# Decoding fp64 weights on chip: a Prelu that carries the sign in bit 28, and a join of one shift

## Chip, cores and metric

The kernel runs on one core of one Trainium2 chip. The metric is the device time of one launch in microseconds (us). Beside it stands one execution recorded by the hardware profiler, with its own time.

## What is computed

An RWKV-6 attention block (4 batches, 8 heads, 768 tokens, head width 48), and on its output a two-layer block with the gate h·erf(softplus(h)):

```python
for t in range(S):
    kt, vt, rt, wt = (k[:, :, t], v[:, :, t], r[:, :, t], w[:, :, t])
    cur = np.einsum('bhd,bhe->bhde', u[None] * kt, vt)
    y[:, :, t] = np.einsum('bhd,bhde->bhe', rt, state + cur)
    state = wt[:, :, :, None] * state + np.einsum('bhd,bhe->bhde', kt, vt)
...
h = x @ w_in                      # 3072 tokens, 384 -> 2048
sp = np.maximum(h, 0.0) + np.log1p(np.exp(-np.abs(h)))
g = h * erf(sp)
return (g @ w_out).astype(np.float32)
```

The two weight matrices arrive as fp64, as the inputs hold them (`w_in` and `w_out` are random numbers divided by a float64 square root), so the kernel turns them into fp32 on the chip.

## The kernel before

**Steps.** The outer loop runs over `n_steps` = 12 steps `s`; each takes 128 tokens of two batches. Step `s` does its attention, and between the pieces of that the two-layer block of earlier steps is put: the first layer of step s-1 (`hidden`, matmuls of L777, whose PSUM tile "m" ScalarE copies out at L786), softplus and erf of it (L759 and L762 for the first steps, L733 and L737 later), and the second layer of step s-3 (`project`, L809, later `project_fast`, L885). The "m" tiles are two, taken in turn: a piece of L777 can start only when the copy L786 of the piece two before it is done.

**Attention of the first steps.** For s < 5 the products inside a block of 64 tokens are built in six levels, `level` 1 to 6. At each level TensorE forms products (L452) into a PSUM tile "pp", VectorE scales the operands for the next level (`scale` at L263), and takes the products into `own` (L668 at level 1, a predicated copy L464 at levels 2 to 5, two ScalarE copies L471 at level 6). Then come a transpose of K (L680), its copy by ScalarE (`kT`, L684), the state's products (L538), additions on VectorE and GpSimd (L710 to L715), and `through_state` (L512 on TensorE, L519 to L522 on ScalarE), whose result `xT` is completed by six small DMAs (L526, three issued by SP, three by ScalarE). The first layer of that step can start when those have landed.

**Order.** The order on each engine is the order in which the program issues (`manual_schedule`). After each level `place(n)` is called, and it puts there what the tables say: pieces of the two-layer block, stages of softplus, erf and their product (`advance`, `STAGES`), and stages of the conversion.

**The conversion.** `convert` is a generator that takes letters. There are 16 pieces of weights, each 128 partitions x 2 x 384: pieces 0 to 7 are `w_in`, 8 to 15 are `w_out`. For one piece i:

- "l", `load(i)`: a 768 KB DMA on SP's queue into a `words` buffer of 32-bit words (3 buffers), the low and the high word of each fp64 next to each other.
- "s", `scale(i)`: ScalarE reads the high words as fp32, multiplies by 2^-112 and writes `base` into the PSUM tile "pp1" (L212); this lowers the exponent field. Then it reads the low words as unsigned integers, multiplies by 2^-29 and writes `rest` (L214, 2 buffers).
- "j", which is `shift` ("h") and then `join` ("o"): VectorE shifts `base` left by 3 bits in place (L220). The sign falls out at the top, so a second VectorE instruction (L228) takes the sign bit from `words`, ors it with the shifted bits and writes the weights. Then GpSimd adds `rest` to them (L232).

`CONVERT` says at which place of which of the steps 0 to 3 which letters run. In step 1 the `h` of piece 2 stands at place 0 ("hl"), and its `o` is issued at level 2 between VectorE's scaling L263 and its taking L464 (`behind(None)`, `BEHIND_SCALING = "os"`). The PSUM tile "pp1" is one: `scale(i+1)` can write it only after VectorE has read piece i out of it. While the conversion runs, all other users of "pp" take "pp0".

Of the kernel before, what the change touches and what calls it, by code (L numbers as in the profile page):

```python
# [11 lines left out]
FP32 = mybir.dt.float32  # L12
I32 = mybir.dt.int32
U32 = mybir.dt.uint32
AF = mybir.ActivationFunctionType
ALU = mybir.AluOpType
# [45 lines left out]
def kernel(  # L62
# [14 lines left out]
    nc = tc.nc  # L77
    PSUM = bass.MemoryType.PSUM

    n_steps, _, _, JP, C = rkw.shape  # L80
# [4 lines left out]
    _, NT, DM = w_out.shape  # L85
# [43 lines left out]
    turns = {"next": 0, "converting": False}  # L129
# [55 lines left out]
    def convert(weights):  # L185

        held = {}

        def load(i):
            if i >= len(weights):
                return
            dst, src = weights[i]
            if src.dtype == FP32:
                nc.sync.dma_start(out=dst, in_=src)
                return
            words = wide.tile([P, 2, DM, 2], I32, name="words", bufs=3)
            nc.sync.dma_start(
                out=words[:].rearrange("p i n two -> p i (n two)"), in_=src.bitcast(I32)  # L200
            )
            held[i] = [words]

        def scale(i):
            if i in held:
                words = held[i][0]
                low, high = words[:, :, :, 0], words[:, :, :, 1]
                base = ps_p.tile([P, 2, NP * C], FP32, name="pp1")[:, :, :DM]
                rest = wide.tile([P, 2, DM], I32, name="rest", bufs=2)


                nc.scalar.mul(out=base, in_=high.bitcast(FP32), mul=2.0**-112)  # L212

                nc.scalar.mul(out=rest[:], in_=low.bitcast(U32), mul=2.0**-29)  # L214
                held[i] += [base.bitcast(I32), rest]

        def shift(i):
            if i in held:
                bits = held[i][1]
                nc.vector.tensor_scalar(  # L220
                    out=bits, in0=bits, scalar1=3, scalar2=None, op0=ALU.logical_shift_left
                )

        def join(i):
            if i in held:
                words, bits, rest = held.pop(i)
                into = weights[i][0].bitcast(I32)
                nc.vector.scalar_tensor_tensor(  # L228
                    out=into, in0=words[:, :, :, 1], scalar=-(1 << 31), in1=bits,
                    op0=ALU.bitwise_and, op1=ALU.bitwise_or,  # L230
                )
                nc.gpsimd.tensor_tensor(out=into, in0=into, in1=rest[:], op=ALU.add)  # L232

        stages = {"l": load, "s": scale, "h": shift, "o": join}
        done = dict.fromkeys(stages, 0)
        for _ in range(3):
            load(done["l"])
            done["l"] += 1
        while True:
            what = yield  # L240
            for stage in {"j": "ho"}.get(what, what):
                stages[stage](done[stage])
                done[stage] += 1
            if weights[0][1].dtype != FP32:
                turns["converting"] = 0 < done["s"] and done["o"] < len(weights)
                turns["next"] = 0

    def rows(e, n=D):
# [723 lines left out]
    def run_late(s, tokens, following=None):  # L972
# [26 lines left out]

    CONVERT = (  # L1000
        ("", "", "", "", "", "s", "jls", "j", "sl"),
        ("hl", "jsl", "jsl", "jsl", "jl", "sj", "", "", "sl"),
        ("jsl", "jsl", "jsl", "jsl", "jl", "sj", "s"),
        ("js", "j"),
    )

    BEHIND_SCALING = "os"

    STAGES = {
        1: (0, 0, 0, 0, 0, 0, 1, 0), 2: (1, 0, 0, 0, 0, 0, 1, 1), 3: (1, 2, 1, 0, 0, 2, 1, 1)  # L1010
# [10 lines left out]
    with tc.manual_schedule(  # L1021
# [9 lines left out]
        for _ in prepare(0):  # L1031
            pass
        conversion = convert(
            [
                (into[:, f : f + 2, :], given[:, f : f + 2, :])
# [6 lines left out]
        for s in range(n_steps):  # L1042
# [39 lines left out]
            def behind(n=0):  # L1082
                if n is not None:
                    convert_at(LOG + 2)
                    return
                for what in BEHIND_SCALING:
                    conversion.send(what)
# [6 lines left out]
        s = n_steps  # L1094
# [104 lines left out]
```

## Time and profile before

| | |
|---|---|
| median of 3 runs | 599.53 us (597.93 to 599.68) |
| the profiled execution, own time | 598.5 us |
| its span | 596.3 us, with 2.2 us around it |
| TensorE (PE) matmuls busy | 584.7 us, 98% |
| VectorE (DVE) busy | 440.1 us, 74% |
| ScalarE (ACT) busy | 361.8 us, 61% |
| GpSimd (POOL) busy | 274.5 us, 46% |
| L212, high words scaled | 16 x 888 ns (median), from 25.4 to 108 us |
| L214, low words scaled | 16 x 915 ns |
| L220, shift | 16 x 966 ns |
| L228, sign and or | 16 x 954 ns |
| L232, GpSimd's addition | 16 x 2.1 to 2.3 us |

A timeline line gives the start, the length, the engine, the source line, the operation, out<-in with the shape, and how many instructions are merged in it; in brackets stands how long the engine was idle before it, and what the profile takes for the releaser. "PEld" is TensorE's loading of weights, "SPq" and "ACTq" are the queues of SP and ScalarE (issues of DMAs). Where several things released a wait, the line names the one that came last before the start, which need not be the true one.

### The profile page before, as it was taken

The page shows a single profiled execution, that of the slowest core. Times are in us where ns is not written, and L with a number is a line of the kernel's source. Part 1 is how long each engine was busy: PE and PEld are TensorE (multiplying, and loading weights), DVE is VectorE, ACT ScalarE, POOL GpSimd, SP SyncE. Part 2 cuts the span into 40 slices and gives each one's busy share as a digit, 9 for nine tenths or more (in the row PEclk, how much of TensorE's full clock was granted, in tenths as well). Part 3 has the DMA queues.
Part 4 walks back from the last instruction along what each step waited for, and adds up shares of the span by engine and source line. Part 5 has one row for each costly group of instructions (what it writes and reads, how often), then busy time and mean ns, then how long its engine had stood idle before and what let it go on. Part 6 is the DMA issues. An engine that isn't in the chain of part 4 may idle for free.

```text
span 596.3 us, 16645 instructions
## 1 busy us (share of the span) xinstructions
PE 584.7 (98%) x7290; PEld 501.7 (84%) x7290; DVE 440.1 (74%) x516; ACT 361.8 (61%) x473; POOL 274.5 (46%) x296
## 2 busy tenths in 40 slices
PE   8889999999999999999999999999999999999997
PEld 7667788678758758898898898898898898898997
DVE  5688598799996799799799799799799525023140
ACT  2547788717534398765765666666666664746710
POOL 4348365610588549749449449449459000000000
PEclk9999999999999999999999999999999999999999
DMA  8377381541315324334334335334331300000000
GB/s 320 124 278 234 118 290 58 217 141 20 134 38 159 66 95 168 71 108 169 72 107 168 73 106 169 73 107 134 71 107 54 71 9 26 2 21 13 2 27 26
DMA packets 51376, 63.33 MB, mean 106 GB/s; under 512 B 34920, under 2 KB 40296, under 8 KB 49896
## 3 DMA queue, kind: packets, MB, share of 16 engines
q1 hardware_dynamic: 50824, 62.03, 32.3%
q8 instruction: 57, 0.93, 0.6%
q10 hardware_dynamic: 480, 0.25, 0.2%
q14 instruction: 15, 0.12, 0.1%
HBM read 52.39 MB, written 8.69 MB: 102 GB/s over the span
## 4 chain that ended last, share of the span: by engine, by line
PE 88%; DVE 6%; issue 2%; ACT 2%; DMA 1%; POOL 1%; SPq 0%; DVEq 0%; ACTq 0%; POOLq 0%
PE m L777 40%; PE m L885 28%; PE m L809 8%; PE pp L452 6%; PE y L486 2%; DVE in L263 2%; PE pp L538 1%; PE y L512 1%; DMA in<-in_rkw 1%; PE pp L680 1%; DVE sums L367 1%; DVE words L381 1%; DVE own L464 1%; ACT rk L292 1%; DVE w_in_sb L228 0%
## 5 line engine op out<-in xcount | busy, mean ns | idle before, releaser
L777 PE MATMUL m<-xT,w_in_sb 128*128 128x256 f32 x1152 | 257.3, 382 | 2.3 <-DVE w_in_sb L228 1.3
L777 PEld LDWEIGHTS m<-xT,w_in_sb 128*128 128x128 f32 x1152 | 216.0, 190 | 34.5 <-issue 3.7
L786 ACT COPY h<-m 128x512 f32<-128x512 f32 x96 | 55.6, 580 | 84.2 <-PE m L777 84.1
L263 DVE TENSOR_TENSOR in<-in,tot_sb 128x1024 f32<-128x1024 f32 (+1 forms) x60 | 78.3, 1305 | 24.9 <-PE pp L452 23.8
L377 POOL TENSOR_TENSOR rk<-words 128x528 f32<-128x528 f32 (+3 forms) x28 | 41.6, 1485 | 91.4 <-DVE sums L367 81.0
L381 POOL TENSOR_TENSOR words<-words,rest 128x528 f32<-128x528 f32 (+10 forms) x77 | 79.1, 1027 | 6.0
L809 PE MATMUL m<-w_out_sb,h 128*128 128x384 f32 x192 | 64.3, 491 | 0.0
L809 PEld LDWEIGHTS m<-w_out_sb,h 128*128 128x128 f32 x192 | 35.7, 190 | 23.6
L885 PE MATMUL m<-mixed,h 128*128 128x192 f32 x288 | 51.1, 331 | 0.0
L885 PE MATMUL m<-w_out_sb,h 128*128 128x192 f32 x288 | 50.3, 329 | 0.0
L733 ACT ACT_TABLE_LOAD x36 | 46.2, 1283 | 2.4 <-issue 1.7
L885 PEld LDWEIGHTS m<-w_out_sb,h 128*128 128x128 f32 x288 | 46.9, 190 | 0.5
L885 PEld LDWEIGHTS m<-mixed,h 128*128 128x128 f32 x288 | 46.6, 190 | 0.9
L737 ACT ACT_TABLE_LOAD x36 | 46.2, 1283 | 1.7 <-DVE room L868 1.1
L452 PEld LDWEIGHTS pp<-in 48*64 48x64 f32 (+1 forms) x2368 | 34.0, 125 | 14.8 <-issue 8.1
L885 PE MATMUL m<-w_out_sb,room 128*128 128x192 f32 x256 | 44.2, 326 | 0.0
L452 PE MATMUL pp<-in 48*64 48x64 f32 (+1 forms) x2368 | 38.7, 212 | 4.0 <-issue 1.8
L315 POOL TENSOR_TENSOR tot_sb<-tot_sb 128x256 f32<-128x256 f32 (+4 forms) x60 | 40.4, 674 | 4.5
L885 PEld LDWEIGHTS m<-w_out_sb,room 128*128 128x128 f32 x256 | 42.0, 190 | 0.0
L742 DVE TENSOR_TENSOR h<-h,y 128x1024 f32<-128x1024 f32 x17 | 20.7, 1215 | 28.3 <-ACT y L737 28.2
L733 ACT ACTIVATE room<-h 128x1024 f32<-128x1024 f32 x36 | 38.1, 1057 | 0.4
L742 DVE TENSOR_TENSOR h<-h,pp 128x1024 f32<-128x1024 f32 x19 | 23.1, 1213 | 19.3 <-ACT pp L737 19.2
(123 smaller groups left out, 826.3 us busy)
## 6 DMA issues: line engine op xcount, KB each, us to landing
in<-in_rkw SPq DMA_DIRECT2D x11, 1024.0 KB, 5.1
words<-in_moe_w_in SPq DMA_DIRECT2D x8, 768.0 KB, 5.5
words<-in_moe_w_out SPq DMA_DIRECT2D x8, 768.0 KB, 4.6
words<-in_rk_rows SPq DMA_DIRECT2D x8, 768.0 KB, 6.2
w<-in_rkw SPq DMA_DIRECT2D x11, 512.0 KB, 7.0
v<-in_v SPq DMA_DIRECT2D x12, 384.0 KB, 6.0
out<-o SPq DMA_DIRECT2D x24, 192.0 KB, 2.4
rest<-in_w_rows SPq DMA_DIRECT2D x8, 384.0 KB, 5.0
```

The costliest lines, as they stand in the source:

```text
L263: nc.vector.tensor_mul(halves, halves, view(tots[level - 1], 0, [[1, n], [2, nb], [0, half]]))
L315: nc.gpsimd.tensor_mul(new, pair[:, :, 0], pair[:, :, 1])
L377: engine.tensor_mul(terms[n], r[:, :, n:], k[:, :, : near - n])
L381: engine.tensor_mul(k[:, :, :m], k[:, :, :m], w[:, :, n : n + m])
L452: nc.tensor.matmul(pp[s0 : s0 + m, e, n, :m], lhsT=rk[rows(e), 1, n, s0 : s0 + m], rhs=rk[rows(e), 0, n, t0 : t0 + m], start=True, stop=True,)
L733: nc.scalar.activation(sp_room, chunks[0], AF.Softplus)
L737: nc.scalar.activation(at, sp_room, AF.Erf)
L742: nc.vector.tensor_mul(h, h, at)
L777: nc.tensor.matmul(ps[:, ff, :], lhsT=w_in_sb[:, g * FG + f + ff, kk * P : (kk + 1) * P], rhs=xT[:, kk, :], start=kk == 0, stop=kk == KT - 1,)
L786: nc.scalar.copy(h[:, f : f + FT, :], ps[:])
L809: nc.tensor.matmul(ps[j][:], lhsT=gs[g][:, f, j * C : (j + 1) * C], rhs=w_out_sb[:, g * FG + f, :], start=g + f == 0, stop=g == NG - 1 and ...
L885: nc.tensor.matmul(to, lhsT=a[:, f], rhs=b[:, f], start=start and f == 0, stop=f == FG - 1, skip_group_check=True,)
```

## The change

Per piece, `scale` writes the high words with the activation function Prelu instead of a plain multiplication: the input is multiplied by 2^-112, positive values pass as they are, negative ones are multiplied by alpha = -2^32. A negative word so becomes a positive number whose exponent field is 32 higher, which sets bit 28. A shift left by 3 then moves bit 28 into the place of the sign. `shift` and the sign-taking instruction go; `join` is one shift that reads "pp1" and writes the weights; `words` is no longer read by VectorE. The letters h and o go, "hl" becomes "l", and "os" becomes "js".

```diff
-                nc.scalar.mul(out=base, in_=high.bitcast(FP32), mul=2.0**-112)
+                nc.scalar.activation(
+                    base, high.bitcast(FP32), AF.Prelu, scale=2.0**-112, alpha=-(2.0**32)
+                )
                 nc.scalar.mul(out=rest[:], in_=low.bitcast(U32), mul=2.0**-29)
                 held[i] += [base.bitcast(I32), rest]
-        def shift(i):
-            if i in held:
-                bits = held[i][1]
-                nc.vector.tensor_scalar(
-                    out=bits, in0=bits, scalar1=3, scalar2=None, op0=ALU.logical_shift_left
-                )
         def join(i):
             if i in held:
-                words, bits, rest = held.pop(i)
+                _, bits, rest = held.pop(i)
                 into = weights[i][0].bitcast(I32)
-                nc.vector.scalar_tensor_tensor(
-                    out=into, in0=words[:, :, :, 1], scalar=-(1 << 31), in1=bits,
-                    op0=ALU.bitwise_and, op1=ALU.bitwise_or,
-                )
+                nc.vector.tensor_scalar(
+                    out=into, in0=bits, scalar1=3, scalar2=None, op0=ALU.logical_shift_left
+                )
                 nc.gpsimd.tensor_tensor(out=into, in0=into, in1=rest[:], op=ALU.add)
-        stages = {"l": load, "s": scale, "h": shift, "o": join}
+        stages = {"l": load, "s": scale, "j": join}
...
-            for stage in {"j": "ho"}.get(what, what):
+            for stage in what:
...
-                turns["converting"] = 0 < done["s"] and done["o"] < len(weights)
+                turns["converting"] = 0 < done["s"] and done["j"] < len(weights)
...
-        ("hl", "jsl", "jsl", "jsl", "jl", "sj", "", "", "sl"),
+        ("l", "jsl", "jsl", "jsl", "jl", "sj", "", "", "sl"),
...
-    BEHIND_SCALING = "os"
+    BEHIND_SCALING = "js"
```

## The prediction, made before the changed kernel was run

> **What bounds the kernel now.** I read first the busy shares and the chain that ended last, on the profile's page:
>
> ```profile
> PE 584.7 (98%) x7290; PEld 501.7 (84%) x7290; DVE 440.1 (74%) x516; ACT 361.8 (61%) x473; POOL 274.5 (46%) x296
> PE 88%; DVE 6%; issue 2%; ACT 2%; DMA 1%; POOL 1%; SPq 0%; DVEq 0%; ACTq 0%; POOLq 0%
> ```
>
> TensorE works 584.7 of 596.3 us and carries 88% of the chain; 11.6 us of the span are left in which it idles. A change on VectorE can pay only there. The conversion lies at 25 to 118 us, so the next view is TensorE's timeline from 30 us on: which gaps it has and what ended them. There are four that matter:
>
> ```profile
> 34.40 3.27 PE L777 MATMUL m<-xT,w_in_sb 128*128 128x256 f32 x12 [1.26 <-DVE w_in_sb L228]
> ...
> 42.33 1.16 PE L452 MATMUL pp<-in 48*64 48x64 f32 x64 [0.77 <-DVE own L464]
> ...
> 69.32 3.14 PE L777 MATMUL m<-xT,w_in_sb 128*128 128x256 f32 x12 [0.98 <-DMA xT<-y]
> ...
> 76.53 1.16 PE L452 MATMUL pp<-in 48*64 48x64 f32 x64 [0.19 <-DVE own L464]
> 77.62 2.86 PE L777 MATMUL m<-xT,w_in_sb 128*128 128x256 f32 x12
> ```
>
> Together 3.2 us (one more, 0.48 us at 51.70, is put down to issue alone). From 77.6 us to the end of TensorE's work there is one more, 0.33 us at 172 us, behind a VectorE chain that itself starts at TensorE's L538 at 146 us: if TensorE comes later, so does that chain. So a delay of TensorE before 77 us reaches the end whole, and so does a gain.
>
> The first gap is put down to the join L228, which ended at 34.28. I don't believe that: this L777 reads piece 0 of the weights, which GpSimd finished at 30.26, and `xT`, whose DMAs were issued at 32.17 and took 1.7 to 2.1 us to land, so about 34.2. The third gap has the same form (issue 67.05, matmul 69.32, 2.27 us; here 2.23 us) and names the DMA.
>
> The last view is ScalarE's timeline about the last gap:
>
> ```profile
> 67.06 2.06 ACTq L526 DMA_DIRECT2D xT<-y  x3
> 69.22 0.86 ACT L212 ACTIVATE pp<-words 128x768 f32<-128x768 f32 x1 [1.92 <-DVE own L668]
> 70.01 0.88 ACT L214 ACTIVATE rest<-words 128x768 int32<-128x768 uint32 x1
> 70.80 0.57 ACT L786 COPY h<-m 128x512 f32<-128x512 f32 x1
> 72.10 0.89 ACT L212 ACTIVATE pp<-words 128x768 f32<-128x768 f32 x1 [0.73 <-DVE w_out_sb L228]
> 72.91 0.92 ACT L214 ACTIVATE rest<-words 128x768 int32<-128x768 uint32 x1
> 73.85 1.28 ACT L762 ACT_TABLE_LOAD   x1
> 75.14 1.91 ACT L762 ACTIVATE room<-room 128x2048 f32<-128x2048 f32 x1
> 76.96 0.57 ACT L786 COPY h<-m 128x512 f32<-128x512 f32 x1
> ```
>
> The copy L786 that ends at 77.53 frees the "m" tile that TensorE's L777 takes at 77.62. There is no slack in that pair: whatever makes this copy late stops TensorE.
>
> **What the Trainium skill says.** "ScalarE: Activation LUTs", section "Table sets: the hidden batching unit": functions are loaded in sets, and the cheap ones found in every set as filler are relu, copy, identity and abs; Prelu is not in that list. Its section "What ACT_TABLE_LOAD costs" gives 1283 ns a load, which is what the 85 loads here show (mean 1283), and 186 + 0.833·N ns for an ACTIVATE with immediate operands plus 93 ns for each per-partition operand: 826 ns for N = 768, against 888 measured for L212. "ScalarE activation tables: per-element evaluation and per-set limits", section "What a function is on this engine": with the same operands an ACTIVATE costs the same whichever table it reads. No run here shows a Prelu. "VectorE: DVE Perf Modes", section "Why PSUM operands drop a tier": an fp32 operation with a PSUM operand runs at one element a cycle. The trace agrees: the shift L220 takes 966 ns for 768 elements.
>
> **Part 1, one VectorE instruction less per piece.** 16 x 954 ns of L228 go, 15.3 us of VectorE. The remaining shift still reads PSUM, so it keeps its 966 ns though it now writes to SBUF; bounds 950 and 1060, the row's shortest and longest. What of it reaches TensorE? *First gap:* nothing, or at most what `xT` leaves, 0.2 us. The chain to `xT` runs kT (L684, 27.27), L538 (28.12), `middle` (L712, to 30.23), L512 (30.49), L519: no join is in it; GpSimd's first addition ends at 29.3 in place of 30.26, and the GpSimd multiplication behind it still waits for `middle`. *Second gap:* nothing. L464 at 40.84 stands behind the scaling at 38.84 and one conversion instruction, the `o` of piece 2 (39.98, 0.95 us). After the change one stands there again, the shift (0.97 us); the other, at 36.47, goes from a place where VectorE then idled 1.41 us. *Third gap:* `xT`, through ScalarE, which is busy without a break from 59.96 (kT, the u products, a table load, softplus): no join in it. *Fourth:* L464 there follows L263 at once, and the join comes after it. From then on TensorE has no gap for a shorter VectorE queue to fill.
>
> **Part 2, waits that get shorter.** ScalarE waited 7.9 us in all for L228 to free "pp1"; 7 waits shrink by up to 0.95 us each. GpSimd's additions start up to 1 us earlier. These are off the path, save one: the 0.73 us ahead of L212 at 72.10.
>
> **Part 3, the words buffers.** They come free after L214 and not after L228, so SP's loads L199 start sooner where SP isn't held by other issues: piece 3's at about 27.3 and not 28.36, piece 5's at about 37.5 (behind the next step's loads) and not 40.99. Behind them on SP stand the `xT` issues and the next step's loads; none is moved past another. When `xT` goes out, at 32.17 and 67.05, piece 3's load is a microsecond further away, piece 4's comes behind the `xT` issues on SP at 34.05 and not 34.31, and piece 10's stays bound by SP's order; so I cost this at nothing. If that cover is gone, an `xT` landing is late by a share of a 768 KB load, below 1 us.
>
> **Part 4, Prelu in place of a multiplication.** Per instruction: 888 ns stays; bounds 0 and +93 ns (if alpha or the bias were read per partition). I take 0, as softplus, with the same default bias, takes 1911 ns for 2048 elements, below the 1986 that a per-partition operand would give. But Prelu needs a table set that holds it. Pieces 0 to 7 run with the table loaded at 0.74 us; pieces 10 to 15 run after an erf and before the next softplus. Pieces 8 and 9 (69.22 and 72.10) run after a softplus (63.82) and before the erf load at 73.85. [...] Bounds: no load (Prelu is in softplus's set too) or one, ahead of piece 8. I take one, since the page's filler list doesn't name Prelu. The load of erf's set at 73.85 stays needed.
>
> Followed through: load 69.13 to 70.41; L212 70.42 to 71.29; L214 71.21 to 72.09; L786 72.00 to 72.57 (TensorE needs that tile at 73.49: covered, 0.9 us to spare). VectorE's shift of piece 8 runs 71.31 to 72.28, so L212 of piece 9 need no longer wait till 72.06 for L228: it runs 72.48 to 73.37, L214 to 74.20, load to 75.50, erf to 77.42, L786 77.33 to 77.90. L777 then starts at 77.99 and not at 77.62: **+0.37 us**. Of the load's delay of 1.20 us to L212, 0.73 us go into the old wait for L228, the rest into the overlap of neighbours. Behind L786 queue the scale of piece 10, which waited until 78.27 before and now can start at 77.8: the delay ends there, and L786 at 79.93 comes earlier than before.
>
> **Sum.** 0 (parts 1 to 3) + 0.37 = +0.37 us: 598.5 to 598.9 us for the profiled execution. The median of the runs stands 1.03 us above that execution, so 599.5 + 0.4 = **599.9 us**. About 0.3%, 1.8 us here, is what a measurement of this kernel can tell from no change.
>
> **Rivals.** *A, no load and a small gain:* Prelu lies in softplus's set, and L228 did hold the first gap. Then TensorE gains at most 34.28 less the landing of `xT`, 0.2 to 1 us: 598.5 to 599.3. For it: the releaser printed at 34.40. Against: the reads of that matmul. *B, a load ahead of piece 0 as well, slower:* if the set loaded at 0.74 for a copy lacks Prelu, a second load sits at 25.41, ahead of L212, L214 and kT (27.27), on which L538, `middle` and `xT` wait with no slack: +1.28 us there, +0.37 at piece 8, and three Prelus on the path at +0.09 each if they read an operand per partition: +1.9 us, 601.4. It decides from the first load on that lies ahead of kT. Against it: pages and trace are silent on which set that is; a set chosen for a copy is likely a general one. *C, Prelu doesn't run at one element a cycle, or reloads at each use:* 16 x 0.9 to 1.3 us on ScalarE, some 5 us at the copies L786, 604 us and more: 20.5 us of loads would fall on a queue that idles 20.6 of the 75 us from 30 to 105 (five windows: 6.22, 11.38, 12.30, 12.43 and 12.10 us busy of 15), and I put a quarter of them through. Against it: the second page. That Prelu's branch doesn't scale exactly would change values and no time. *D, a gain above 1.8 us:* it would need over half of the 3.2 us, of which VectorE holds 0.96; I see no mechanism.
>
> **How the numbers follow.** Forecast 0.62, A 0.18, B 0.11, C 0.05, D 0.04. Faster than 597.7: D and a scatter of medians of 0.1 to 0.2%, 0.09. Slower than 601.3: most of B, C, and scatter, 0.17. Within: 0.74. The range 598.3 to 601.5 holds the forecast, A and B with the scatter, and leaves out C and D and the tails.
>
> **What would show it.** DVE busy down by 15 us to 425 with 500 instructions; L220 and L228 gone, one shift of about 966 ns writing the weights; Prelu rows at about 888 ns; 86 ACT table loads and not 85, the new one at 69.1 ahead of piece 8; PE's L777 at about 78.0 with a wait for L786; gaps at 34.4, 42.3 and 69.3 unchanged. Wrong would be: a load near 25.4, Prelu rows above 980 ns, the gap at 34.40 shrinking by over 0.3 us, or new waits for `xT`.

## The result and the profile after

The change is slower. Its median is 601.38 us (8 runs) against 598.79 us of the kernel before beside it (8 runs); the ratio is 1.005, 95% interval 1.0029 to 1.0071, which is +3.0 us (1.7 to 4.3). The forecast was +0.4.

The profiled execution took 605.16 us, with a span of 603.4 us. It is the longest of the eight, and it starts late: the first L771 (L777 before) comes at 38.17 us and not at 34.40. Its page shows TensorE at six tenths of its clock in the second of 40 slices; read in steps of 1 or 2 us, the granted clock is 0.50 from 19 to 28 us. A second profile of the same kernel (602.73 us) starts it at 35.72.

This is not particular to the change. There are fourteen profiles in this case. In six of them, one of the kernel before among them, the first L777 starts at 35.72 us or later; each of these has a stretch in its first 28 us in which the granted clock is 0.50, and a mean granted clock over the whole execution of 0.990 to 0.997. The other eight start it between 34.40 and 34.87 us, with a mean of 0.999 or 1.000. I call these *executions at full clock*.

So I don't compare spans, but the *stage* of the conversion: from the start of the first L771 to the start of the first matmul of the second layer (L803, L809 before). That is 70.71 us after (38.17 to 108.88), and 71.00 in the second profile (35.72 to 106.72), against 67.70 before (34.40 to 102.10).

The page after, lines of its parts 1, 2 and 4:

```profile
PE 588.3 (97%) x7290; PEld 503.5 (83%) x7290; DVE 433.1 (72%) x500; ACT 362.9 (60%) x474; POOL 273.5 (45%) x296
PEclk9699999999999999999999999999999999999999
PE 82%; DVE 9%; ACT 5%; issue 2%; DMA 1%; ACTq 0%; POOL 0%; SPq 0%; DVEq 0%; POOLq 0%
```

VectorE has its 16 instructions less, but its busy time fell by 7.0 us and not by 15.3, and its share of the chain grew from 6% to 9%. Something on VectorE became longer: the scalings, 78.3 us in all before and 86.1 after. TensorE's timeline after shows where it hurts; the scaling is L257 now (L263 before), the taking L458 (L464), the level products L446 (L452):

```profile
38.17 3.30 PE L771 MATMUL m<-xT,w_in_sb 128*128 128x256 f32 x12 [1.22 <-DMA xT<-y]
46.13 1.16 PE L446 MATMUL pp<-in 48*64 48x64 f32 x64 [0.78 <-DVE own L458]
50.57 1.40 PE L446 MATMUL pp<-in 48*64 48x64 f32 x64 [0.49 <-DVE own L458]
55.12 1.16 PE L446 MATMUL pp<-in 48*64 48x64 f32 x64 [0.37 <-DVE own L458]
59.61 0.75 PE L446 MATMUL pp<-in 48*32 48x32 f32 x64 [0.54 <-DVE own L458]
74.17 3.14 PE L771 MATMUL m<-xT,w_in_sb 128*128 128x256 f32 x12 [0.98 <-DMA xT<-y]
81.64 1.16 PE L446 MATMUL pp<-in 48*64 48x64 f32 x64 [0.45 <-DVE own L458]
86.09 1.16 PE L446 MATMUL pp<-in 48*64 48x64 f32 x64 [0.37 <-DVE own L458]
90.63 1.16 PE L446 MATMUL pp<-in 48*64 48x64 f32 x64 [0.59 <-DVE own L458]
95.13 0.74 PE L446 MATMUL pp<-in 48*32 48x32 f32 x64 [0.55 <-DVE own L458]
```

The gaps ahead of the two L771 and of level 3 of step 1 (0.78) are those of before. New are seven waits for L458, ahead of levels 4 to 6 of step 1 and 3 to 6 of step 2: 3.36 us, where before stood 0.67 (0.48, put down to issue, and 0.19). The difference, 2.69 us, is nearly all of the 3.0 us by which this stage grew.

Why L458 is late is on VectorE's timeline of the change, here at level 3 of step 1 (L223 is the one shift):

```profile
45.79 0.98 DVE L223 TENSOR_SCALAR w_in_sb<-pp 128x768 int32<-128x768 int32 x1
47.35 2.47 DVE L257 TENSOR_TENSOR in<-in,tot_sb 128x1024 f32<-128x1024 f32 x1 [0.58 <-PE pp L446]
49.74 0.68 DVE L458 COPY_PREDICATED own<-mask_sb,pp 128x512 f32<-128x512 int32 x1
```

and on GpSimd's timeline of the change at the same time (L226 is the addition):

```profile
46.91 1.82 POOL L226 TENSOR_TENSOR w_in_sb<-w_in_sb,rest 128x768 int32<-128x768 int32 x1 [0.20 <-DVE w_in_sb L223]
```

The same place before, from VectorE's timeline:

```profile
43.07 0.95 DVE L228 SCALAR_TENSOR_TENSOR w_in_sb<-words,pp 128x768 int32<-128x768 int32 x1
43.95 1.22 DVE L263 TENSOR_TENSOR in<-in,tot_sb 128x1024 f32<-128x1024 f32 x1
45.08 0.73 DVE L464 COPY_PREDICATED own<-mask_sb,pp 128x512 f32<-128x512 int32 x1
45.70 0.96 DVE L220 TENSOR_SCALAR pp<-pp 128x768 int32<-128x768 int32 x1
```

and from GpSimd's:

```profile
44.17 2.67 POOL L232 TENSOR_TENSOR w_in_sb<-w_in_sb,rest 128x768 int32<-128x768 int32 x1 [1.27 <-DVE w_in_sb L228]
```

Read the second column. Before, the scaling starts first and takes 1.22 us, and the addition beside it takes 2.67. After, the addition starts 0.44 us ahead, takes 1.82, and the scaling takes 2.47: it ends at 49.82, 1.09 us after the addition's end at 48.73, much as if it had only begun there. So the two don't share; the later one waits. The other six long scalings after end in the same way, 1.08 or 1.09 us behind the end of the addition beside them. What decides who is first is the VectorE instruction that went: before, VectorE ran shift, sign-and-or and scaling back to back, so that the addition, released by the sign-and-or, came 0.2 us behind the scaling's start at four levels and 0.02 us behind it at a fifth. Now VectorE is done early, idles 0.58 us until TensorE is ready for the scaling, and in that hole GpSimd begins.

The Trainium skill, "SBUF — State Buffer", section "SBUF: two separate sides", says this outright: VectorE and GpSimd share a pair of ports as an exclusive lock. Of a VectorE instruction with two SBUF inputs and a GpSimd instruction that reads SBUF, the one that starts first holds it to its end, and the other is blocked. The scaling reads `in` and `tot_sb`, both in SBUF. The trace agrees, with the numbers above. And two VectorE instructions that don't have two SBUF inputs did run beside an addition: the taking at 45.08 and the shift at 45.70 us before, which read PSUM, keep 0.73 and 0.96 us beside the addition that runs from 44.17 to 46.84.

The table load stands where it was expected, once, ahead of piece 8 (ScalarE's timeline of the change; L780 is the copy L786 of before):

```profile
74.04 1.28 ACT L212 ACT_TABLE_LOAD   x1 [1.91 <-issue]
75.34 0.86 ACT L212 ACTIVATE pp<-words 128x768 f32<-128x768 f32 x1
82.25 0.57 ACT L780 COPY h<-m 128x512 f32<-128x512 f32 x1
```

The copy ends at 82.82, while the level products ahead of the matmul that needs it end at 82.80. It costs next to nothing here, because those products are late anyhow.

### The profile page after: what moved, and what is told of

Same layout as the page of the kernel before. It is cut to its first block, busy times and chain, and to the rows that moved or that the text cites. A ratio compares the mean times of both kernels' runs of the same rounds, so it can differ in the third digit from the quotient of the medians.

```text
span 603.4 us, 16621 instructions
## 1 busy us (share of the span) xinstructions
PE 588.3 (97%) x7290; PEld 503.5 (83%) x7290; DVE 433.1 (72%) x500; ACT 362.9 (60%) x474; POOL 273.5 (45%) x296
## 4 chain that ended last, share of the span: by engine, by line
PE 82%; DVE 9%; ACT 5%; issue 2%; DMA 1%; ACTq 0%; POOL 0%; SPq 0%; DVEq 0%; POOLq 0%
PE m L771 36%; PE m L879 28%; PE pp L446 6%; PE m L803 4%; DVE in L257 4%; PE y L480 2%; PE y L506 1%; PE pp L532 1%; DVE own L458 1%; PE y L632 1%; PE pp L674 1%; DMA in<-in_rkw 1%; ACT room L727 1%; DMA xT<-y 1%; DVE sums L361 1%
## 5 line engine op out<-in xcount | busy, mean ns | idle before, releaser
L771 PE MATMUL m<-xT,w_in_sb 128*128 128x256 f32 x1152 | 257.6, 382 | 2.3 <-DMA xT<-y 2.2
L771 PEld LDWEIGHTS m<-xT,w_in_sb 128*128 128x128 f32 x1152 | 216.0, 190 | 34.9 <-issue 4.0
L257 DVE TENSOR_TENSOR in<-in,tot_sb 128x1024 f32<-128x1024 f32 (+1 forms) x60 | 86.1, 1436 | 34.3 <-PE pp L446 33.2
L780 ACT COPY h<-m 128x512 f32<-128x512 f32 x96 | 55.6, 580 | 85.4 <-PE m L771 85.3
L803 PE MATMUL m<-w_out_sb,h 128*128 128x384 f32 x192 | 64.3, 491 | 0.0
L803 PEld LDWEIGHTS m<-w_out_sb,h 128*128 128x128 f32 x192 | 35.7, 190 | 23.6
L446 PEld LDWEIGHTS pp<-in 48*64 48x64 f32 (+1 forms) x2368 | 35.7, 131 | 18.0 <-PE m L771 7.1
L446 PE MATMUL pp<-in 48*64 48x64 f32 (+1 forms) x2368 | 40.2, 218 | 6.8 <-DVE own L458 4.1
```

Of the source, the lines that this page charges most:

```text
L257: nc.vector.tensor_mul(halves, halves, view(tots[level - 1], 0, [[1, n], [2, nb], [0, half]]))
L446: nc.tensor.matmul(pp[s0 : s0 + m, e, n, :m], lhsT=rk[rows(e), 1, n, s0 : s0 + m], rhs=rk[rows(e), 0, n, t0 : t0 + m], start=True, stop=True,)
L771: nc.tensor.matmul(ps[:, ff, :], lhsT=w_in_sb[:, g * FG + f + ff, kk * P : (kk + 1) * P], rhs=xT[:, kk, :], start=kk == 0, stop=kk == KT - 1,)
L780: nc.scalar.copy(h[:, f : f + FT, :], ps[:])
L803: nc.tensor.matmul(ps[j][:], lhsT=gs[g][:, f, j * C : (j + 1) * C], rhs=w_out_sb[:, g * FG + f, :], start=g + f == 0, stop=g == NG - 1 and ...
```

## The experiments

Three theories. **P**: the additions on GpSimd and the scalings on VectorE meet, and whoever starts first holds up the other. **T**: the table load and what it delays on ScalarE. **M**: the words buffers come free earlier, so that SP's loads start earlier and disturb other transfers. Each ratio is to the runs of before on the same chip, with its 95% interval; 0.001 is 0.6 us. "Stage" is the time from the first L771 to the first L803 in the one profile of each kernel; three profiles of before (the one shown and two more, below) give 67.70, 67.41 and 67.01. The column "full clock" compares medians of executions at full clock alone, with the number of those of the kernel in the row; it is needed because the share of the others differs between the kernels (5 of 39, 8 of 35 and 10 of 35 of before, but 13 of 22, 6 of 10 and 5 of 8 of three others).

| kernel | ratio | in us | full clock, us | stage | scalings above 1.6 us in steps 1 and 2 |
|---|---|---|---|---|---|
| the change | 1.0050 (1.0029 to 1.0071) | +3.0 | not on record | 70.71, 71.00 | 7 |
| two shifts, Prelu | 1.0045 (1.0026 to 1.0064) | +2.7 | +2.1 (3) | 69.97 | 2 |
| one shift, no Prelu | 1.0054 (1.0031 to 1.0077) | +3.2 | +2.9 (6) | 70.15 | 6 |
| the change without the addition | 0.9995 (0.9982 to 1.0009) | -0.3 | 0.0 (11) | 67.51 | 1 (1.71) |
| the change, addition behind the scaling | 1.0019 (1.0011 to 1.0026) | +1.1 | +1.2 (19) | 68.79 | 0 |
| two shifts, no Prelu | 1.0018 (1.0006 to 1.0029) | +1.1 | +1.4 (8) | 68.68 | 1 |
| before, with Prelu | 1.0033 (1.0023 to 1.0044) | +2.0 | +1.5 (4) | 68.37 | 1 |
| all mended | 1.0017 (1.0008 to 1.0027) | +1.0 | +0.5 (9) | 67.47 | 0 |
| two shifts, no Prelu, piece 5 held | 1.0013 (1.0004 to 1.0023) | +0.8 | +0.7 (12) | 68.13 | 0 |
| before, piece 5 held | 1.0006 (0.9993 to 1.0019) | +0.4 | -0.1 (8) | 67.03 | 0 |

For the change itself the clocks of the runs of before beside it are not on record. If its four shortest, 597.77 to 598.05 us, were those at full clock, the change costs 3.4 us there (an estimate: 601.34 less 597.89).

**The change without the addition.** The weights lack their low words.

```diff
-                nc.gpsimd.tensor_tensor(out=into, in0=into, in1=rest[:], op=ALU.add)
```

> The change without GpSimd's addition of the low words (they are left out of the weights). Theory P: nothing on GpSimd can hold the scaling, it takes 1.2 us at each level, TensorE's gaps at levels 3 to 6 go; -0.3 to +0.4 us against before. Theory T and theory M: +2.6 us, as the change.

Measured 0.9995 (0.9982 to 1.0009). The Prelu, the load, the single shift and the early loads are all there, and the time is that of before. So neither the load nor the early loads of the words cost the 3 us by themselves; what is left to them is to act through the addition, and the kernels below take that apart. The one longer scaling fits P too: it starts at 82.03, inside a product on GpSimd that runs from 81.83 to 82.66, and ends 1.08 us behind it. The kernel also shows the load's own price, in the one gap that is new on TensorE's timeline (L779 is the copy):

```profile
78.01 2.86 PE L770 MATMUL m<-xT,w_in_sb 128*128 128x256 f32 x12 [0.55 <-ACT h L779]
```

**One shift, no Prelu.** The weights lack their signs.

```diff
-                nc.scalar.activation(
-                    base, high.bitcast(FP32), AF.Prelu, scale=2.0**-112, alpha=-(2.0**32)
-                )
+                nc.scalar.mul(out=base, in_=high.bitcast(FP32), mul=2.0**-112)
```

> The change with the plain multiplication in place of the Prelu, so with one shift and no extra table load; the weights lose their sign, so the result is not the reference's. Theory P: TensorE's gaps stay, +2.2 to +2.7 us against before. Theory T: no load, so 0 against before. Theory M: +2.6 us.

Measured 1.0054, +3.2 us. The missing VectorE instruction is enough, with no load: six scalings take 2.42 to 2.54 us, as in the change.

**The change with the addition behind the scaling.** `join` puts the addition on a list; after the next scaling it is issued, behind a copy of one element that the scaling wrote:

```diff
             scale(s, level)
+            half = 1 << (level - 1)
+            add_up(in_t[:, 0, 0, half : half + 1])
```

`add_up` copies 128x1 elements on GpSimd and then issues the additions on the list.

> The change with GpSimd's addition put behind the next level's scaling in steps 1 and 2: it is issued after it, behind a copy of one element a partition that reads what the scaling wrote. The load of the table, the Prelu and the single shift stay, nothing is left out. Theory P: the scaling takes 1.2 us, the addition 1.83 us in VectorE's shadow, the gaps of levels 3 to 6 go; 0 to +0.8 us against before (a weight piece may be late by a few tenths in step 1). Theory T and theory M: +2.6 us, as the change.

Measured 1.0019, +1.1 us, a little above the expected 0 to 0.8. At level 3 of step 2, from VectorE's timeline of it and from GpSimd's:

```profile
77.84 1.23 DVE L268 TENSOR_TENSOR in<-in,tot_sb 128x1024 f32<-128x1024 f32 x1 [0.65 <-PE pp L457]
```

```profile
79.34 1.81 POOL L192 TENSOR_TENSOR w_out_sb<-w_out_sb,rest 128x768 int32<-128x768 int32 x1
```

All scalings take 1.22 to 1.53 us, and of the 3 us two are back. The rest is in three gaps of TensorE: 0.57 for the copy behind the table load, 0.23 for a weight piece that comes late, and 0.65 at the start of step 3, where VectorE waits for a GpSimd product queued behind two additions that took 5.66 us together beside two-operand VectorE work.

**Two shifts, Prelu.** The shift by 3 is split: by 1 in place, by 2 into the weights, so that the addition is released as late as before.

```diff
+                nc.vector.tensor_scalar(out=bits, in0=bits, scalar1=1, scalar2=None, op0=ALU.logical_shift_left)
-                    out=into, in0=bits, scalar1=3, scalar2=None, op0=ALU.logical_shift_left
+                    out=into, in0=bits, scalar1=2, scalar2=None, op0=ALU.logical_shift_left
```

> The change with its Prelu, but the shift made in two VectorE instructions: left by 1 in place in PSUM, where the old shift stood, and left by 2 into the weights, where the old sign-and-or stood. GpSimd's addition so starts as late behind the next level's scaling as in the kernel before. Theory P (GpSimd's addition now starts ahead of VectorE's two-operand scaling, and the scaling waits for it): the scaling at levels 3 to 6 of steps 1 and 2 takes 1.2 us again, GpSimd's addition 2.7 us, TensorE's gaps of 0.4 to 0.6 us there go; 0 to +0.5 us against before, about 2.2 us faster than the change. Theory T (the table load and ScalarE's delays behind it): as slow as the change, +2.6 us. Theory M (the earlier loads of the words buffers, which this kernel keeps, disturb other transfers): as slow as the change.

Measured 1.0045, +2.7 us, where P as I had put it expected at most 0.5. The scalings at the usual places are back at 1.22 us, but two others run into an addition: 2.77 us at level 2 of step 2, with a gap of 1.44 us on TensorE, and 2.62 us at level 5 of step 1. So the load does something that I had left out, and there is a second near meeting. The next two kernels take these apart.

**Before, with Prelu.** Only the load is added.

```diff
-                nc.scalar.mul(out=base, in_=high.bitcast(FP32), mul=2.0**-112)
+                nc.scalar.activation(base, high.bitcast(FP32), AF.Prelu, scale=2.0**-112, alpha=1.0)
```

> The kernel before with the high words scaled by a Prelu of slope 1, which gives the values of the plain multiplication; shift, sign-and-or and all places stay. It only adds the table load ahead of piece 8 and what follows from it. Theory P: the load moves the addition of piece 8 by about 1.3 us to just before the scaling at level 2 of step 2, which then takes 2.5 to 2.8 us, with a TensorE gap of 1.2 to 1.4 us at level 3: +1.0 to +2.0 us against before. Theory T0 (the load costs only what the prediction gave it, the late copy L786): +0.3 to +0.6 us and a scaling of 1.2 to 1.5 us there. Theory R (a Prelu is slower than a multiplication): the rows of L212 are above 980 ns and the first gap comes later by 0.1 us or more.

Measured 1.0033, +2.0 us. GpSimd's timeline of it, and then VectorE's:

```profile
74.45 1.82 POOL L234 TENSOR_TENSOR w_out_sb<-w_out_sb,rest 128x768 int32<-128x768 int32 x1 [7.99 <-DVE w_out_sb L230]
```

```profile
74.58 2.78 DVE L265 TENSOR_TENSOR in<-in,tot_sb 128x1024 f32<-128x1024 f32 x1 [0.27 <-PE pp L454]
77.28 1.32 DVE L466 COPY_PREDICATED own<-mask_sb,pp 128x512 f32<-128x512 int32 x1
```

The same two instructions before, from GpSimd's timeline and from VectorE's:

```profile
72.21 1.83 POOL L232 TENSOR_TENSOR w_out_sb<-w_out_sb,rest 128x768 int32<-128x768 int32 x1 [6.70 <-DVE w_out_sb L228]
```

```profile
73.63 1.49 DVE L263 TENSOR_TENSOR in<-in,tot_sb 128x1024 f32<-128x1024 f32 x1 [1.56 <-PE pp L452]
```

The load pushes the addition of piece 8 from 1.42 us ahead of the scaling to 0.13 us ahead of it, so the scaling waits for nearly all of it; TensorE's gap at level 3 is 1.44 us instead of 0.19. Those 1.25 us are most of what the load costs at full clock, +1.5 us; the +2.0 us of the ratio are larger, as six of the ten executions were not at full clock. In the change both edits act on that addition and partly cancel: its join is one instruction shorter, it stands 1.14 us ahead (77.33 and 78.47), and the scaling takes 1.77 us. TensorE's gap at this place is 1.44 us with the load alone, none with one shift alone, and 0.45 in the change. So the two parts, +1.5 and +2.9 us at full clock, don't add up to the whole.

**Two shifts, no Prelu.** Both edits are undone as to their times; only the earlier loads of the words buffers stay. The weights lack their signs. Against the kernel with two shifts and Prelu:

```diff
-                nc.scalar.activation(... AF.Prelu ...)
+                nc.scalar.mul(out=base, in_=high.bitcast(FP32), mul=2.0**-112)
```

> Two shifts as in the kernel with 1 and 2 bits, but the plain multiplication in place of the Prelu: no extra table load; the weights lose their sign, so the result is not the reference's. The words buffers are still freed by ScalarE, so SP's loads start as early as in the change. Theory P (GpSimd's additions and VectorE's scalings meet, and whoever starts first holds the other up): both things that move the additions, the missing VectorE instruction and the table load, are gone, so the scalings take 1.2 us, the gaps of 0.4 us and more go, -0.3 to +0.4 us against before. Theory M (the earlier loads of the words buffers): +2.6 us, as the change.

Measured 1.0018, +1.1 us (0.4 to 1.7): neither theory's number. Its timeline of all engines at level 5 of step 1:

```profile
52.33 0.34 PE L451 MATMUL pp<-in 48*64 48x64 f32 x6 [0.75 <-issue]
52.47 1.82 POOL L231 TENSOR_TENSOR w_in_sb<-w_in_sb,rest 128x768 int32<-128x768 int32 x1
52.73 2.65 DVE L262 TENSOR_TENSOR in<-in,tot_sb 128x1024 f32<-128x1024 f32 x1 [1.09 <-PE pp L451]
...
56.13 0.75 PE L451 MATMUL pp<-in 48*32 48x32 f32 x64 [0.68 <-DVE own L463]
```

and that of before at the same place:

```profile
51.70 0.34 PE L452 MATMUL pp<-in 48*64 48x64 f32 x6 [0.48 <-issue]
...
52.10 1.23 DVE L263 TENSOR_TENSOR in<-in,tot_sb 128x1024 f32<-128x1024 f32 x1 [0.82 <-PE pp L452]
52.12 2.88 POOL L232 TENSOR_TENSOR w_in_sb<-w_in_sb,rest 128x768 int32<-128x768 int32 x1
```

In the kernel before the scaling wins by 0.02 us; here the last six products came 0.27 us later by TensorE's own issue, and it lost.

**The same, with the addition of piece 5 held** behind that scaling, as above but for this one:

```diff
+            turns["hold"] = (s, level) == (1, 4)
             place(level - 1)
```

> The kernel with two shifts and the plain multiplication (signs lost, as there), with one addition more put in a fixed place: that of piece 5 is issued behind the scaling of level 5 in step 1, by a copy of one element that reads what the scaling wrote. Theory P (the +1.3 us of that kernel come from the addition of piece 5, which may start just ahead of the scaling): the scaling takes 1.2 us in every execution, the gap of 0.7 us at level 6 goes; a late weight piece may cost 0.2 to 0.3 us; -0.2 to +0.6 us against before. Theory M (the earlier loads of the words buffers): still +1.3 us.

Measured 1.0013, +0.8 us (0.2 to 1.4). The scaling takes 1.23 us and the gap of 0.68 us is gone. At full clock the loss fell from 1.4 to 0.7 us, as much as the gap; by the ratios alone the fall is smaller than the interval. So some 0.7 or 0.8 us remain in a kernel that differs from before by the earlier loads, the held piece and a second shift in place of the sign-and-or; what they are is open. The gap "issue" of 0.75 us at level 5 of step 1 stands in both profiles of the two-shift kernels without Prelu, and one of 0.80 in that with Prelu, against 0.48, 0.21 and none in three of before. The earlier loads alone don't bring it: the change and the change without the addition have them too, and have no such gap there.

**Before, with piece 5 held.** The same edit on the kernel before.

> The kernel before, with the addition of piece 5 put behind the scaling of level 5 in step 1 in the same way. Theory P: the executions of before in which that addition starts first are gone; -0.4 to +0.3 us against before, and a narrower scatter. Theory N (the 0.02 us between the two starts does not matter): +0.2 us, from the late weight piece, with the same scatter.

Measured 1.0006 (0.9993 to 1.0019): no difference, and the scatter is as wide (597.68 to 601.99). So the near meeting does not make the scatter of before. The clock goes with it: the eight executions at full clock lie between 597.68 and 598.51, the six from 599.08 up have a mean granted clock of 0.991 to 0.997. Of the 35 of before beside them, the 25 at full clock have a median of 598.10, the ten others of 599.47.

**All mended.** The addition held at levels 2 to 4 (step 1) and 1 to 4 (step 2), pieces 8 and 9 made as before so that no load is needed, piece 2 joined at place 0 of step 1:

```diff
+                if i in (8, 9):
+                    nc.scalar.mul(out=base, in_=high.bitcast(FP32), mul=2.0**-112)
...
-        ("l", "jsl", "jsl", "jsl", "jl", "sj", "", "", "sl"),
+        ("jl", "jsl", "jsl", "jsl", "jl", "sj", "", "", "sl"),
-    BEHIND_SCALING = "js"
+    BEHIND_SCALING = "s"
```

> A version that should beat both: the change with GpSimd's addition held behind the next scaling at levels 2 to 4 of step 1 and 1 to 4 of step 2; pieces 8 and 9, which fall between softplus and erf, made as before (multiplication, shift, sign-and-or), so that no table load is added; and piece 2 joined at place 0 of step 1, not between the scaling and the taking of level 2. Theory P: no table load, no scaling above 1.6 us, the gap of 0.77 us at level 3 of step 1 gone: -1.0 to 0 us against before. Theory M: +2 us.

Measured 1.0017 (1.0008 to 1.0027), +1.0 us, where -1.0 to 0 was expected. In the profile every gap aimed at is gone, the 0.77 us at level 3 of step 1 too, and the stage takes 67.47 us, inside the range of before. So it gives back two thirds of the loss, and there is no version here that beats the kernel before. Half of its last microsecond is a matter of the clock: 13 of its 22 executions were not at full clock, against 8 of 35 of before; whether the kernel itself brings that about is open. At full clock +0.5 us remains. The profile can't show where it lies, as it is of an execution of 598.44 us, one of this kernel's shortest.

**Second and third profiles.**

> The change once more, unaltered, for a second profile: the first one is of its longest execution (605.16 us against a median of 601.38), with TensorE at 0.6 of its clock for a while near 20 us. Theory P: the gaps of 0.4 to 0.6 us ahead of levels 3 to 6 of steps 1 and 2 stand again, the start to the first L771 takes about 35 us and not 38, the span is about 599.5.

602.73 us, span 600.9. The seven gaps stand again, 0.34 to 0.61 us, behind scalings of 2.33 to 2.55 us and one of 1.78: they are no accident of the first profile. The span is not the 599.5 expected: this execution too was not at full clock (0.997).

> The kernel before once more, for its spread: either the profile shown again (first L777 at 34.4, gaps 0.77 and 0.19), or one of its executions above 599 us, which should then show either a later start (36 us) or a scaling of 2.6 us at level 5 of step 1 with a gap of 0.7 us behind it.

> As the run before it: the kernel before, a third profile, to see how far the start to the first L777 and the meeting at level 5 of step 1 vary.

599.15 and 599.61 us. The first is neither of the two cases expected: at full clock, the first L777 starts at 34.63, and the extra time lies behind the stage (494.96 us from there to the end, against 494.20). In it another GpSimd instruction, a product of L315 from 51.81 to 52.42, holds up the scaling of level 5, which starts at 52.08 and takes 1.42 us: it ends again 1.08 us behind the other's end. The second is the expected late start: with a mean granted clock of 0.997, the first L777 starts at 36.24 us, 1.8 us later than in the profile shown, with a stage of 67.01.

## Why the prediction was wrong, point by point

- **What bounds the kernel**: right. TensorE's gaps between 34 and 77 us were read rightly; the first is the wait for `xT` (after, the line names the DMA), and it is 1.22 us, against 1.26 before.
- **Part 1**: right in its parts (16 instructions of 954 ns gone, the shift at 952 and 949 ns on average), and right that the shorter queue closed none of the four gaps listed; the fourth grew from 0.19 to 0.45 us.
- **Part 2 is the step that failed**: "GpSimd's additions start up to 1 us earlier. These are off the path". At levels 3 to 6 no wait of TensorE is put down to them, but the scaling of the next level waits for them by the lock. An addition that moves from 0.2 us behind a scaling's start to 0.4 us ahead of it makes the scaling 1.2 us longer; TensorE, which had about 0.7 us of slack there (50.09 against 49.43 for the end of L464), loses 0.4 to 0.6 us each time. The prediction said that from 77 us on there is no gap that a shorter VectorE queue could fill, and took that for safety; it did not ask what an earlier start elsewhere could run into.
- **The sign was in the view of before.** The addition's row there had a shortest, median and longest duration of 1817, 2251 and 2882 ns, for one shape. Each long one between 34 and 86 us had started beside a running scaling. The table of the kernel before gives only the medians, "2.1 to 2.3 us", and the prediction asked no further. Its rivals on the slower side were a second table load and a slow Prelu; the lock was in no rival.
- **A right number by luck.** Rival B said 601.4 us, and the median is 601.38. But nothing of B came about: no load near 25 us, no Prelu that takes longer. Of the four signs named as showing the prediction wrong none appeared either; what showed it was VectorE's busy time, 433.1 us and not 425. Its forecast of 599.9 rested on a median of three runs, 599.53; the eight beside the change gave 598.79, so +0.4 against +3.0 is the fairer comparison.
- **Part 3**: by themselves the earlier loads cost nothing that shows (the change without the addition has them, 0.0 us at full clock). Whether they have a share in the 0.7 or 0.8 us that stay open in the two-shift kernel with piece 5 held is not shown.
- **Part 4**: right on the load, its place (74.04, after ScalarE's DMA issues) and its number, and on the Prelu's price (mean 877 ns in the change, 893 in the kernel before with Prelu, against 886). Its own cost at the copy was 0.37 by the sum and 0.55 where nothing else hides it. But the sum left out that it also moves the addition of piece 8 to just ahead of a scaling: by itself, in the kernel before, the load costs +2.0 us, or +1.5 at full clock, and this one meeting makes a TensorE gap 1.25 us longer.

## What to carry to other kernels

When an instruction on VectorE goes, list what it was holding back, not only what waits for it: a GpSimd instruction released earlier can start ahead of a two-operand VectorE instruction and stop it for its whole length. Look in the profile for one GpSimd or VectorE group, of one shape, with two durations, and compare the starts of its long ones with what the other engine runs: the order of the two starts says who paid. Two durations alone don't prove a meeting. The predicated copy takes 1.32 or 1.33 us at level 2 and 0.70 to 0.73 later in the kernel without the addition too, with GpSimd idle at level 2 of step 1 (41.26 us). Where such an order matters, it is better made by a dependence than left to 20 ns.

## What the runs showed of the hardware that was not expected

An integer addition of 128x768 on GpSimd and a 128x1024 product of two SBUF operands on VectorE exclude each other: 1.82 and 1.22 us alone, 2.67 for the addition if it starts second (44.17), 2.47 for the product if it does (47.35). The held products end about 1.1 us behind what held them. A shift from PSUM and a predicated copy into SBUF ran beside an addition at their usual 0.95 and 0.7 us. Executions of the kernel before differ by up to 1.8 us in the start of the first L777 (34.40, 34.63 and 36.24 us), and the late one is the one whose granted clock drops to 0.50, near 12 us. In all six late profiles TensorE had waited 1.2 to 1.9 us just ahead of such a drop. But it waited as long, 1.23 and 1.29 us near 16 us, in both two-shift kernels without Prelu, at full clock throughout; what brings the drop is open.
